# Two of five weight products of a transformer block taken from three fp32r passes to one fp32 pass

## The chip, the cores and the metric

The kernel runs on one core of a Trainium2 chip. Its engines work side by side, each through its own instructions in order: TensorE (PE in the profile, its weight loads PEld), VectorE (DVE), ScalarE (ACT), GpSimd (POOL), and SyncE (SP), which issues the DMAs. The metric is device microseconds (us) of one execution; less is better. Three runs of the kernel before took 1993.77, 1999.7 and 2000.05 us, so the median is 1999.7 us.

## The reference

The program is a block with modulated layer norms, 2048 tokens, width 512, all in fp32: attention with 32 heads of 16, then a mixer of two perceptrons with a token shift between its first two products. Cut to what matters:

```python
mod = (_silu(c) @ w_mod).reshape(c.shape[0], 6, 1, -1)
sa, ca, ga, sb, cb, gb = (mod[:, 0], mod[:, 1], mod[:, 2], mod[:, 3], mod[:, 4], mod[:, 5])
h = _layernorm(x) * (1 + ca) + sa
x = x + ga * attention(h, A_wqkv, A_wo)       # 32 heads of 16, softmax over 2048 keys
h = _layernorm(x) * (1 + cb) + sb
x = x + gb * mixer(h)

# mixer(x):
h = _gelu(_layernorm(x) @ w1)                 # 512 -> 512
g0, g1, g2, g3 = the four quarters of h's 512 columns, shifted by +1, -1, +2, -2 tokens
x1 = x + concatenate([g0, g1, g2, g3]) @ w2   # 512 -> 512
return x1 + _gelu(_layernorm(x1) @ w3) @ w4   # 512 -> 1792 -> 512
```

## The kernel before

**Attention.** The 2048 queries are taken in four chunks of 512. A chunk has 16 units (a unit is a pair of heads), and a unit has 16 steps, one for each 128 keys: 1024 steps in all. A step does two products for the scores (`sc`, line L1021), whose exponent ACT takes into the tile `pt` (L1017); two products for the row maxima of a unit that comes 24 steps later (`mb`, L1005), which DVE reduces (`mx`, L1001); a pass by POOL over `pt` that makes its low part (L1072, sometimes two halves on ACT instead); and the products with the values (`pv`, L1098 and L1095). Seven PSUM banks are shared by `sc`, `mb` and everything else but `pv`.

**The tail of a chunk** is all that follows attention: `tail(ci)`. It multiplies by `wo`, adds the residual, does two layer norms, then `mix1` (product with w1 and GELU into the tile `g1`), `mix2` (product with w2 over the token-shifted `g1`, the residual and a layer norm), and last the groups of `FG`: for each group of 128-column blocks of w3, the product with w3 and GELU into the tile `g2`, then for each 128-token tile one sum of products with w4 over the blocks of that group, which DVE adds to `x1` (L1535). A group's sum is one PSUM bank. Because of the shift by up to two tokens, the tail of chunk 0 finishes 3 token tiles, those of chunks 1 and 2 finish 4 each and that of chunk 3 finishes 5: 16 tiles. For each of these, w2 has 4 blocks and w4 has 14, so there are 16 x 18 = 288 products of 128x128 by 128x512 with w2 and w4.

**Three passes.** An fp32 product is made of three fp32r matmuls (`mm3`, L339, L341, L343) of operands that are split into a high and a low part: high by high, high by low, low by high. Activations are split behind the GELU: ACT rounds the GELU's result `xs` to the high part (L1427), POOL subtracts that for the low part (L1428). Weights are split once, while attention runs over the first chunk: `pieces_load` brings 40 tiles of 128x512 of wo, w1, w2, w3 and w4 from the inputs, `pieces_gen` scales them (w2 and w4 by 0.5, w4 also by a modulation row), splits them (ACT L900, POOL L902 or DVE L901), and stores both parts to `Ws`. A tail reads them back through `Ring`, three tiles `wr` of 1 MB ahead, 20 loads for each chunk.

**What sets the order.** `Sched` writes the instructions of all engines in one fixed order while the program is built, with its own clocks of the engines. Attention is written block by block of three pairs of row products. After every second block `fill` lets waiting generators (the tails, and during the first chunk the products for queries, keys and values) emit PE work, up to a budget of ns for each step: 900 and 700 in the first chunk, then the entries of `TAILB` for chunks 1, 2 and 3. So the tails of chunks 0, 1 and 2 are emitted between the blocks of attention of the following chunk, and the tail of chunk 3 comes after attention, alone. The list `chains` holds the elementwise work on ACT, DVE and POOL that belongs to a product; `misc` puts it between attention's own work on these engines. PE, DVE, ACT and POOL wait for each other by semaphores alone.

Of the kernel before, what the change touches and what calls it, by code (L numbers as in the profile page):

```python
# [15 lines left out]
OP = mybir.AluOpType  # L16
# [22 lines left out]
TAILB = (0.0, 500.0, 560.0, 590.0)  # L39
# [271 lines left out]
def kernel(ctx, tc, A_x, A_wqkv, A_wo, B_w1, B_w2, B_w3, B_w4, c, w_mod, out):  # L311
# [70 lines left out]
    FG = [(0, 4), (4, 4), (8, 4), (12, 2)]  # L382
# [93 lines left out]
    zero = con.tile([4, CH], F32, name="zero")  # L476
# [381 lines left out]
    def pieces_load():  # L858
        yield lambda: ("kq", 1) in done
        for i, (nm, src, nk, n) in enumerate(pieces):  # L860
# [12 lines left out]
    def pieces_gen():  # L873
        while True:
            yield lambda: loaded and wqs
# [4 lines left out]
            w = wqs.pop(0)  # L880
# [19 lines left out]
            sch.chain(*ops, ("A", cA(), lambda f=f, w=w: act.activation(w, f, AF.Copy)),  # L900
                      ("D", 2 * cD(), lambda f=f, t=t, w=w: dve.tensor_tensor(t, f, w, op=OP.subtract)) if nm in rows and c else  # L901
                      ("G", cG(), lambda f=f, t=t, w=w: pool.tensor_tensor(t, f, w, op=OP.subtract)),  # L902
                      (None, 0, store), ready=e)
# [58 lines left out]
    def load_unit(u):  # L962
# [4 lines left out]
        if u > 2:  # L967
            sch.dma(dma.dma_start, q[0::32].bitcast(F32), zero)
# [151 lines left out]
    def o_fin(u, ac, ready):  # L1120
# [9 lines left out]
        sm = at.tile([P, 8, DH + 1], F32, name="sm", tag="sm", bufs=1)  # L1130
        rc = at.tile([P, 8, 1], F32, name="rc", tag="rc", bufs=2)
# [22 lines left out]
    class Ring:  # L1154
# [9 lines left out]
        def add(self, n, pl=0):  # L1164

            for _ in range(n):
                if self.n < len(self.ids):
# [3 lines left out]
                    e = sch.dma(dma.dma_start, w.bitcast(F32), Ws[i])  # L1171
                    self.q.append((halves(w, pieces[i][2]), pl, e + WLAT))
# [50 lines left out]

    def cols_mm(b, w, i, A, n):
# [6 lines left out]
    def tail(ci):  # L1231
# [12 lines left out]
        if not rings:  # L1244
            ids = order["wo"] + order["w1"] + order["w2"]
            for f0, nf in FG:
                ids = ids + order["w3"][f0 // 2:(f0 + nf) // 2] + order["w4"][f0 // 2:(f0 + nf) // 2]
            rings.append(Ring(ids * NC))
# [18 lines left out]

        if ci:
# [139 lines left out]
        def gelu(b, n, hi, lo, key):  # L1408
            live.append(key)
            xs, sq = [tp[n > 2 * P].tile([P, 3 * P if n > 2 * P else 2 * P], F32, name=nm, tag=nm, bufs=XB) for nm in ("xs", "sq")]  # L1410
            xs, sq = xs[:, :n], sq[:, :n]
# [8 lines left out]
            def prod():  # L1420
                dve.scalar_tensor_tensor(xs, sq, 1.0, b, op0=OP.add, op1=OP.mult)  # L1421
# [4 lines left out]
                      ("D", cD(n), prod),  # L1426
                      ("A", cA(n), lambda: act.activation(hi, xs, AF.Copy)),  # L1427
                      ("G", cG(n), lambda: pool.tensor_tensor(lo, xs, hi, op=OP.subtract)), (None, 0, end), bank=b)  # L1428
# [274 lines left out]
```

## Time and profile before

| | |
|---|---|
| median of three runs | 1999.7 us (1993.77 to 2000.05) |
| profiled execution, span from first to last instruction | 2000.7 us, 1.0 us above the median |
| PE | 1920.9 us busy, 96% |
| POOL | 1676.1 us, 84% |
| DVE | 1652.2 us, 83% |
| ACT | 1473.6 us, 74% |
| DMA | 46.4% of 16 engines' time, 147 GB/s |
| granted TensorE clock, mean | 0.986 |

The profile gives no other time for the profiled execution than its span. PE's busy time is the time covered by at least one matmul from its start to its modelled end; matmuls overlap, so a stretch without a gap is not yet PE at its peak, and the distance from one start to the next tells more than the duration. L numbers are lines of the kernel; L339, L341 and L343 are the helper `mm3`, so there the tiles tell which product it is: `w<-wr,g` are w2 and w4, `w<-A,wr` are w1 and w3.

### The profile page before, as it was taken

The numbers are of one execution on the slowest core, as the hardware profiler recorded it, in microseconds if no ns is written. First come the engines' busy times: TensorE is split into PE (matmuls) and PEld (weight loads), VectorE is DVE, ScalarE is ACT, GpSimd is POOL, SyncE is SP. The second block draws the span as 40 slices with busy tenths as digits, with TensorE's granted clock in tenths as the row PEclk, the third lists the DMA queues.
The fourth block names the chain that finished last, engine by engine and source line by source line (L and its number), as shares of the span: only waits on it lengthen the run. The fifth ranks groups of instructions, "written<-read, shape, count | busy, mean of one in ns | idle before, by whom it ended". The sixth has DMA issues, their size and how long they took to land.

```text
span 2000.7 us, 42354 instructions
## 1 busy us (share of the span) xinstructions
PE 1920.9 (96%) x14480; PEld 1146.7 (57%) x14480; DVE 1652.2 (83%) x3010; ACT 1473.6 (74%) x3083; POOL 1676.1 (84%) x1609
## 2 busy tenths in 40 slices
PE   7999999999999999999999999999999999999899
PEld 4655555555455555555455555555555555555798
DVE  7887988888899888888989898898898889883643
ACT  5376888777878777777878787786787878777443
POOL 6287999889999998888999998898899989888532
PEclk8999999999999999999999999999999999999999
DMA  5767677766643334345433333334433343334432
GB/s 184 205 201 228 182 231 218 244 225 192 198 157 111 115 103 143 109 136 162 126 111 92 109 111 114 115 119 148 157 98 100 115 151 107 121 95 147 149 146 90
DMA packets 232352, 293.24 MB, mean 147 GB/s; under 512 B 125876, under 2 KB 177076, under 8 KB 215848
## 3 DMA queue, kind: packets, MB, share of 16 engines
q1 hardware_dynamic: 232136, 290.53, 46.4%
q8 instruction: 115, 1.88, 0.4%
q14 instruction: 101, 0.83, 0.1%
HBM read 225.81 MB, written 62.91 MB: 144 GB/s over the span
## 4 chain that ended last, share of the span: by engine, by line
PE 67%; DVE 16%; ACT 8%; issue 3%; POOL 2%; DMA 2%; SPq 1%; POOLq 0%; ACTq 0%; DVEq 0%
PE mb L1005 14%; PE sc L1021 10%; PE pv L1098 10%; DVE mx L1001 9%; PE w L339 7%; PE w L343 6%; PE w L341 6%; PE pv L1095 4%; ACT pt L1017 4%; POOL pt L1072 2%; DVE xs L1421 1%; DVE sq L1418 1%; DMA vst<-Vs 1%; PE mr L644 1%; PE ot L1127 1%
## 5 line engine op out<-in xcount | busy, mean ns | idle before, releaser
L1072 POOL TENSOR_SCALAR pt<-pt 128x1024 f16<-128x1024 uint16 x988 | 1312.5, 1365 | 132.6 <-ACT pt L1017 125.4
L1001 DVE TENSOR_REDUCE mx<-mb 128x1 f32<-128x512 f32 x2048 | 1281.0, 683 | 76.0 <-PE mb L1005 54.5
L1017 ACT ACTIVATE pt<-sc 128x512 int32<-128x512 f32 x2048 | 1090.8, 606 | 272.3 <-PE mb L1005 164.9
L1005 PE MATMUL mb<-kst,qtl 64*128 64x512 f32 x2048 | 752.1, 454 | 49.0 <-ACT pt L1017 16.1
L1021 PE MATMUL sc<-qtl,kst 64*128 64x512 f32 x2048 | 716.4, 444 | 2.6 <-DVE A L329 0.6
L1005 PEld LDWEIGHTS mb<-kst,qtl 64*128 64x128 f32 x2048 | 348.7, 193 | 254.5 <-DVE mx L1001 91.4
L1021 PEld LDWEIGHTS sc<-qtl,kst 64*128 64x128 f32 x2048 | 335.6, 186 | 153.5 <-DVE mx L1001 47.1
L1098 PE MATMUL pv<-pt,vst 128*32 128x512 f16 x4096 | 358.2, 397 | 0.1
L1095 PE MATMUL pv<-pt,vst 128*17 128x512 f16 (+1 forms) x2048 | 213.7, 394 | 2.2 <-POOL pt L1072 1.7
L1098 PEld LDWEIGHTS <-vst 128*32 128x32 bf16 x4096 | 90.9, 95 | 167.6 <-issue 108.8
L339 PE MATMUL w<-A,wr 128*128 128x256 f32 (+2 forms) x576 | 175.3, 304 | 0.3 <-ACT A L333 0.3
L1428 POOL TENSOR_TENSOR g<-xs,g 128x256 fp32r<-128x256 f32 (+2 forms) x144 | 103.2, 718 | 83.4 <-ACT g L1427 81.3
L341 PE MATMUL w<-A,wr 128*128 128x256 f32 (+2 forms) x576 | 169.8, 295 | 0.5 <-DVE A L329 0.3
L343 PE MATMUL w<-A,wr 128*128 128x256 f32 (+2 forms) x576 | 167.7, 291 | 0.0
L339 PEld LDWEIGHTS w<-A,wr 128*128 128x128 f32 x576 | 109.6, 190 | 35.4 <-DVE mx L1001 10.3
L339 PE MATMUL w<-wr,g 128*128 128x512 f32 x288 | 119.2, 414 | 0.6 <-ACT g L1427 0.6
L341 PEld LDWEIGHTS w<-A,wr 128*128 128x128 f32 x576 | 109.9, 191 | 12.4 <-issue 11.3
L343 PE MATMUL w<-wr,g 128*128 128x512 f32 x288 | 114.7, 398 | 0.2 <-POOL g L1428 0.2
L341 PE MATMUL w<-wr,g 128*128 128x512 f32 x288 | 113.6, 394 | 0.0
L343 PEld LDWEIGHTS w<-A,wr 128*128 128x128 f32 x576 | 109.8, 191 | 6.7 <-issue 6.7
L1535 DVE TENSOR_TENSOR x<-x,w 128x512 f32<-128x512 f32 x64 | 43.9, 687 | 82.0 <-PE w L343 82.0
L1424 ACT ACTIVATE sq<-w 128x256 f32<-128x256 f32 (+2 forms) x144 | 55.7, 387 | 68.8 <-PE w L343 66.0
(151 smaller groups left out, 2103.8 us busy)
## 6 DMA issues: line engine op xcount, KB each, us to landing
wr<-Ws SPq DMA_DIRECT2D x80, 1024.0 KB
kst<-Ks SPq DMA_DIRECT2D x189, 256.0 KB
vst<-Vs SPq DMA_DIRECT2D x252, 192.0 KB
qtl<-Qs SPq DMA_DIRECT2D x192, 64.0 KB
Vs<-vt SPq DMA_DIRECT2D x32, 384.0 KB
Ws<-wq SPq DMA_DIRECT2D x40, 256.0 KB
Ws<-wst SPq DMA_DIRECT2D x40, 256.0 KB
wst<-in_B_w_dram SPq DMA_DIRECT2D x36, 256.0 KB
```

Source lines behind the costliest of these rows:

```text
L339: te.matmul(o, lh, rh, start=first, stop=False)
L341: te.matmul(o, lh, rl, start=False, stop=False)
L343: te.matmul(o, ll, rh, start=False, stop=last)
L1001: end = sch.crit("D", 605, e + PX, lambda: dve.reduce_max(mxs[u][:, j, g, c:c + 1], b, axis=AX.X))
L1005: return ready, lambda: te.matmul(b, lhs, kst[u % 3][r, c * CH:(c + 1) * CH], start=True, stop=True), after
L1017: ea = sch.crit("A", 480, e + PX, lambda: act.activation(pt[s][:, j], b, AF.Exp))
L1021: return ready, lambda: te.matmul(b, kst[u % 3][r, kt * P:(kt + 1) * P], qst[u][r], start=True, stop=True), after
L1072: e_low[s] = XP["G"] + sch.crit("G", 1345, ready, lambda: pool.tensor_scalar(o, i, 0.5, 1.0, op0=OP.mult, op1=OP.mult))
L1095: te.matmul(acc[r:r + n, :], v[:, (kt + i) % 4, c - n:c].bitcast(F16), pt[s + i].bitcast(F16)[:, j, 0::2], start=False, stop=kt == NKT - 2 ...
L1098: te.matmul(acc[r:r + 32, :], v[:, kt % 4, r:r + 32], pt[s].bitcast(F16)[:, j, 1::2], start=kt == 0, stop=False, skip_group_check=True)
L1424: sch.chain(("A", cA(n), lambda: act.activation(sq, b, AF.Square)), ("D", cD(n), cube), ("A", cA(n), lambda: act.activation(sq, sq, AF.Tan ...
L1428: ("G", cG(n), lambda: pool.tensor_tensor(lo, xs, hi, op=OP.subtract)), (None, 0, end), bank=b)
```

## The change

The products with w2 and w4 become one fp32 matmul instruction in the program each (`plain_mm`, which advances the builder's clock by 3.75 times that of one 512-column fp32r matmul), over operands that are not split. GELU's last DVE operation writes straight into `g1` or `g2`; its copy on ACT and its subtraction on POOL are gone, and `g1` and `g2` hold one part where they held two. The weights of w2 and w4 are scaled, not split, and stored once; a ring load then holds four 128-row blocks where it held two, so a chunk takes 16 loads. The sums with w4 run over groups of 8 and 6 blocks, in the last chunk 4, 4 and 6, where they ran over 4, 4, 4 and 2. The entries of `TAILB` are 94 ns higher. Within a group, the w3 products of the token groups are taken in turn by pairs of blocks. Smaller edits: the tiles `sm` and `rc` behind attention have one buffer more, and the DMA that clears rows of a query tile reads a tile of 128 columns four times over. Products with wo, w1, w3, the queries, keys and values keep their three passes.

```diff
-TAILB = (0.0, 500.0, 560.0, 590.0)
+TAILB = (0.0, 594.0, 654.0, 684.0)
...
-    FG = [(0, 4), (4, 4), (8, 4), (12, 2)]
+    FG = [[(0, 8), (8, 6)]] * (NC - 1) + [[(0, 4), (4, 4), (8, 6)]]
+    PLAIN = ("w2", "w4")
...
-        for k0 in range(0, w.shape[0], 2 * P):
+        step = (4 if nm in PLAIN else 2) * P
+        for k0 in range(0, w.shape[0], step):
             order[nm].append(len(pieces))
-            pieces.append((nm, w[k0:k0 + 2 * P], 2, D))
+            x = w[k0:min(k0 + step, w.shape[0])]
+            pieces.append((nm, x, x.shape[0] // P, D))
...
-    zero = con.tile([4, CH], F32, name="zero")
+    zero = con.tile([4, P], F32, name="zero")
...
             def store(i=i, c=c, w=w, f=f, gone=gone, nm=nm):
-                for h, t in enumerate((w.bitcast(F32), f)):
-                    e = sch.dma(dma.dma_start, Ws[i][:, h, 512 * c:512 * c + 512], t)
+                if w is None:
+                    e = sch.dma(dma.dma_start, flat(Ws[i])[:, c], f)
+                else:
+                    for h, t in enumerate((w.bitcast(F32), f)):
+                        e = sch.dma(dma.dma_start, Ws[i][:, h, 512 * c:512 * c + 512], t)
...
-            if nm in ("w2", "w4"):
+            if plain:
                 ops.append(("A", cA(), lambda f=f: act.activation(f, f, AF.Copy, scale=0.5)))
-            sch.chain(*ops, ("A", cA(), lambda f=f, w=w: act.activation(w, f, AF.Copy)),
-                      ("D", 2 * cD(), lambda f=f, t=t, w=w: dve.tensor_tensor(t, f, w, op=OP.subtract)) if nm in rows and c else
-                      ("G", cG(), lambda f=f, t=t, w=w: pool.tensor_tensor(t, f, w, op=OP.subtract)),
-                      (None, 0, store), ready=e)
+            if not plain:
+                ops += [("A", cA(), lambda f=f, w=w: act.activation(w, f, AF.Copy)),
+                        ("D", 2 * cD(), lambda f=f, t=t, w=w: dve.tensor_tensor(t, f, w, op=OP.subtract)) if nm in rows and c else
+                        ("G", cG(), lambda f=f, t=t, w=w: pool.tensor_tensor(t, f, w, op=OP.subtract))]
+            sch.chain(*ops, (None, 0, store), ready=e)
...
-        sm = at.tile([P, 8, DH + 1], F32, name="sm", tag="sm", bufs=1)
-        rc = at.tile([P, 8, 1], F32, name="rc", tag="rc", bufs=2)
+        sm = at.tile([P, 8, DH + 1], F32, name="sm", tag="sm", bufs=2)
+        rc = at.tile([P, 8, 1], F32, name="rc", tag="rc", bufs=3)
...
+    def plain_mm(b, lhs, w, ks, nk):
+
+        for k in ks:
+            te.matmul(b, lhs(k), w[k // 4][:, k % 4], start=k == 0, stop=k == nk - 1)
+            yield 3.75 * nsq(CH)
...
-                pool.tensor_copy(g[:, k, :, 0:130], g[:, k, :, CH:CH + 130])
-            sch.chain(*[("G", 990, partial(copy, k)) for k in range(KT)], mark(("g", ci)))
+                pool.tensor_copy(g[:, k, 0:130], g[:, k, CH:CH + 130])
+            sch.chain(*[("G", 500, partial(copy, k)) for k in range(KT)], mark(("g", ci)))
...
-                dve.scalar_tensor_tensor(xs, sq, 1.0, b, op0=OP.add, op1=OP.mult)
+                dve.scalar_tensor_tensor(dst, sq, 1.0, b, op0=OP.add, op1=OP.mult)
                 sch.free(b)
...
-                      ("D", cD(n), prod),
-                      ("A", cA(n), lambda: act.activation(hi, xs, AF.Copy)),
-                      ("G", cG(n), lambda: pool.tensor_tensor(lo, xs, hi, op=OP.subtract)), (None, 0, end), bank=b)
+                      ("D", cD(n), prod), (None, 0, end), bank=b)
...
-                    yield from rows_mm(b, lambda k, p: g[:, k, p, 130 + (t - t0) * P - SH[k]:][:, :P], w, range(KT), KT)
+                    yield from plain_mm(b, lambda k: g[:, k, 130 + (t - t0) * P - SH[k]:][:, :P], w, range(KT), KT)
...
-                    yield from rows_mm(b, lambda k, p: g2[si][:, k, p, i * P:(i + 1) * P], w, range(nf), nf)
+                    yield from plain_mm(b, lambda k: g2[si][:, k, i * P:(i + 1) * P], w, range(nf), nf)
```

The builder's order moves with it. First, the tail of the third chunk (chunk 2), at a visit of PE to the sums with w4 between two blocks of attention, in the first group. `sc` and `mb` are attention's row products, `w` is the bank of the sum, `wr` the weights, `g` the tile g2. Before:

```order
L1005 MATMUL mb<-kst_153,qtl_151 128x512 x2
L1021 MATMUL sc<-qtl_605,kst_607 128x512 x2
L1005 MATMUL mb<-kst_153,qtl_151 128x512
L339 MATMUL w_24728<-wr,g_23769 128x512
L341 MATMUL w_24728<-wr,g_23769 128x512
L343 MATMUL w_24728<-wr,g_23769 128x512
```

The three last rows are one block of w4, and they come four times over in this visit, a whole sum of 4 blocks. Now, in the same tail and group:

```order
L1017 MATMUL mb<-kst_149,qtl_147 128x512
L1033 MATMUL sc<-qtl_770,kst_772 128x512 x2
L1017 MATMUL mb<-kst_603,qtl_601 128x512 x2
L1033 MATMUL sc<-qtl_770,kst_772 128x512
L1244 MATMUL w_24449<-wr,g_23008 128x512 x5
L1033 MATMUL sc<-qtl_770,kst_772 128x512
```

Five of the 8 blocks of one sum stand together, one instruction each, and the sum goes on in later visits.

Second, POOL in the same tail while `mix1` runs: its pass over `pt`, the subtraction for g1's low part (L1428), and small operations of attention (`nm`, `osb`). Before:

```order
L1428 TENSOR_TENSOR g_8517<-xs,g_8517 128x256
L1072 TENSOR_SCALAR pt_615<-pt_615 128x1024
L1072 TENSOR_SCALAR pt_616<-pt_616 128x1024
L1072 TENSOR_SCALAR pt_617<-pt_617 128x1024
L1428 TENSOR_TENSOR g_8517<-xs,g_8517 128x256
L1072 TENSOR_SCALAR pt_618<-pt_618 128x1024
```

Now, in the same stage of that tail:

```order
L1150 TENSOR_TENSOR osb<-sm,rc 128x4x32
L1084 TENSOR_SCALAR pt_613<-pt_613 128x1024
L1084 TENSOR_SCALAR pt_614<-pt_614 128x1024
L1084 TENSOR_SCALAR pt_615<-pt_615 128x1024
L1084 TENSOR_SCALAR pt_616<-pt_616 128x1024
L1084 TENSOR_SCALAR pt_609<-pt_609 128x1024
L1066 TENSOR_TENSOR nm<-mf,nm 128x8
```

The subtractions between the passes over `pt` are gone and nothing stands in their place.

Third, PE at the end of the program, where the last block of w3 (`A` by `wr`, 384 tokens) meets the last sums with w4. Before:

```order
L339 MATMUL w_29493<-A,wr 128x384
L341 MATMUL w_29493<-A,wr 128x384
L343 MATMUL w_29493<-A,wr 128x384
L339 MATMUL w_29513<-wr,g_29434 128x512
L341 MATMUL w_29513<-wr,g_29434 128x512
L343 MATMUL w_29513<-wr,g_29434 128x512
```

Behind these, the five tiles' sums take 2 blocks each, 30 matmuls. Now:

```order
L343 MATMUL w_28332<-A,wr 128x384
L1244 MATMUL w_28350<-wr,g_28133 128x512 x6
L1244 MATMUL w_28361<-wr,g_28133 128x512 x6
L1244 MATMUL w_28370<-wr,g_28134 128x512 x6
L1244 MATMUL w_28379<-wr,g_28134 128x512 x6
L1244 MATMUL w_28388<-wr,g_28134 128x512 x6
```

The five tiles' sums take 6 blocks each, 30 products; the two tiles whose GELUs come first (`g_28133`) stand ahead of the three that read the last GELU's tile (`g_28134`).

More of the change, by code (lines that the diff above doesn't have):

```diff
@@ L865, in pieces_load @@
             src3 = kpn(src)
-            for c in range(2):
+            for c in range(nk if nm in PLAIN else 2):
                 yield sch.wait(PLOAD)
                 yield lambda: len(wst) > WSR or len(ready) + ready["done"] > len(todo)
-                t, _, e = yield from staged([src3[:, c:c + 1] if nk == 2 else src3[:, 2 * c:2 * c + 2]])
+                t, _, e = yield from staged([src3[:, 2 * c:2 * c + 2] if n < D else src3[:, c:c + 1]])
                 loaded.append((i, nm, c, t, e))
@@ L874, in pieces_gen @@
         while True:
-            yield lambda: loaded and wqs
+            yield lambda: loaded and (loaded[0] is None or loaded[0][1] in PLAIN or wqs)
             x = loaded.pop(0)
@@ L879, in pieces_gen @@
             i, nm, c, t, e = x
-            w = wqs.pop(0)
+            plain = nm in PLAIN
+            w = None if plain else wqs.pop(0)
             f = t.bitcast(F32)
@@ L1244, in tail @@
         if not rings:
[L1245 to L1248, printed above, removed]
+            ids = []
+            for groups in FG:
+                ids += order["wo"] + order["w1"] + order["w2"]
+                for f0, nf in groups:
+                    ids += order["w3"][f0 // 2:(f0 + nf) // 2] + order["w4"][f0 // 4:(f0 + nf + 3) // 4]
+            rings.append(Ring(ids))
         ring = rings[0]
@@ L1493, in tail @@
             yield from mix1(0, grp[0])
-            w, more = yield from ring.get(2)
+            w, more = yield from ring.get(1)
             yield from mix2(0, sub[0])
@@ L1501, in tail @@
                 yield from mix1(gi, ts)
-            w, more = yield from ring.get(2)
+            w, more = yield from ring.get(1)
             for si, ts in enumerate(sub):
@@ L1505, in tail @@
         more()
-        for fi, (f0, nf) in enumerate(FG):
-            g2 = []
+        for fi, (f0, nf) in enumerate(FG[ci]):
+            g2 = [tG(nf, len(ts) * P) for ts in sub]
             w3 = []
-            for si, ts in enumerate(sub):
-                n = len(ts) * P
-                g2.append(tA("g2", n))
+            turns = [(fl, si) for fl in range(0, nf, 2) for si in range(len(sub))]
+            if end and not fi:
+                turns.sort(key=lambda x: x[1])
+            for fl, si in turns:
+                n = len(sub[si]) * P
                 yield lambda: ("T4", ci, si) in done
-                for fl in range(nf):
-                    if len(w3) <= fl // 2:
-                        w3.append((yield from ring.get(1)))
-                    (w,), more = w3[fl // 2]
+                if len(w3) <= fl // 2:
+                    w3.append((yield from ring.get(1)))
+                (w,), more = w3[fl // 2]
+                for i in range(2):
                     yield wait_bank
                     b = dbank("w3")
-                    yield from cols_mm(b[:, :n], w, fl % 2, An["xn4", si], n)
-                    gelu(b[:, :n], n, g2[si][:, fl, 0, :n], g2[si][:, fl, 1, :n], ("g2", ci, si, f0 + fl))
-                    if fl % 2 and si == len(sub) - 1:
-                        more()
-            w, more = yield from ring.get(nf // 2)
-            if fi == len(FG) - 1:
+                    yield from cols_mm(b[:, :n], w, i, An["xn4", si], n)
+                    gelu(b[:, :n], n, g2[si][:, fl + i, :n], ("g2", ci, si, f0 + fl + i))
+                if si == len(sub) - 1:
+                    more()
+            w, more = yield from ring.get((nf + 3) // 4)
+            if fi == len(FG[ci]) - 1:
                 done.add(("last", ci))
```

37 lines of the change are left out of this document (24 added, 13 removed).

## The prediction

> **What bounds the kernel now.** I read the page's head and its chain of waits first, to see which engine the end hangs on.
>
> ```profile
> span 2000.7 us, 42354 instructions
> PE 1920.9 (96%) x14480; PEld 1146.7 (57%) x14480; DVE 1652.2 (83%) x3010; ACT 1473.6 (74%) x3083; POOL 1676.1 (84%) x1609
> PE 67%; DVE 16%; ACT 8%; issue 3%; POOL 2%; DMA 2%; SPq 1%; POOLq 0%; ACTq 0%; DVEq 0%
> ```
>
> PE is covered for 96% of the span and holds two thirds of the chain. But 96% counts each matmul to its modelled end, so it hides short waits; and three other engines stand at 74 to 84%. So the second view is the table of windows, cut at the stages: attention over the four chunks, the latency stretch behind it, and the last tail.
>
> ```profile
> core 0: us, PE busy (x) PEld busy (x) DVE busy (x) ACT busy (x) POOL busy (x), PEclk, DMA share, GB/s
> 104.90:562.20 457.30, 436.90 (x3289) 242.54 (x3287) 384.04 (x653) 364.30 (x752) 408.09 (x347) 0.98 0.70 213
> 562.20:991.80 429.60, 415.86 (x3319) 234.73 (x3318) 377.47 (x699) 332.96 (x709) 383.14 (x371) 0.99 0.41 128
> 991.80:1422.00 430.20, 420.51 (x3353) 241.48 (x3356) 380.65 (x701) 336.53 (x705) 390.55 (x371) 1.00 0.37 115
> 1422.00:1845.80 423.80, 415.49 (x3313) 240.67 (x3312) 350.21 (x650) 332.38 (x697) 383.46 (x370) 1.00 0.38 119
> 1845.80:1892.00 46.20, 39.93 (x218) 32.47 (x215) 27.96 (x66) 19.27 (x41) 25.40 (x44) 0.93 0.43 162
> 1892.00:2000.70 108.70, 104.87 (x583) 94.01 (x581) 47.84 (x92) 40.32 (x91) 34.75 (x43) 1.00 0.33 120
> ```
>
> The last 109 us are PE alone: the others stand below half. In chunks 1 to 3 (562 to 1846), where the tails of chunks 0 to 2 run, POOL is at 0.89 to 0.91 and DVE at 0.83 to 0.88, so there the balance of four engines sets the pace. The third view, the waits, says what PE meets there.
>
> ```profile
> PEld mb L1005 <- DVE mx L1001: 91.4, 221, 3.8
> PEld mb L1005 <- ACT pt L1017: 82.0, 197, 1.4
> PE pv L1095 <- POOL pt L1072: 1.7, 3, 0.9
> ```
>
> Row products wait for banks that DVE's reductions and ACT's exponents give back; PE hardly ever waits for POOL directly.
>
> **The price of a product.** Three passes, from the timeline near the end, where PE is never held up:
>
> ```profile
> 1990.20 0.39 PE L339 MATMUL w<-wr,g 128*128 128x512 f32 x1
> 1990.43 0.39 PE L341 MATMUL w<-wr,g 128*128 128x512 f32 x1
> 1990.65 0.39 PE L343 MATMUL w<-wr,g 128*128 128x512 f32 x1
> 1990.88 0.39 PE L339 MATMUL w<-wr,g 128*128 128x512 f32 x1
> ```
>
> From start to start a pass takes 0.23 us, so a product 0.69. The kernel already has plain fp32 products, for other ends:
>
> ```profile
> 43.90 0.60 PE L795 MATMUL vb<-qk,gcol 128*128 128x256 f32 x2
> 44.33 0.60 PE L596 MATMUL tr<-ident,xt 128*128 128x128 f32 x4
> ...
> L795 PE MATMUL vb<-qk,gcol x16: 377/379/382, 41.1 to 188.1; 128*128 128x256 f32 x16
> ...
> L550 PE MATMUL mr<-wm,sil x16: 592/592/1057, 5.6 to 14.8; 128*1 128x512 f32 x16
> ...
> L339 PEld LDWEIGHTS w<-wr,g x288: 186/188/192, 676.2 to 1996.0; 128*128 128x128 f32 x144
> L339 PE MATMUL w<-wr,g x288: 387/393/507, 676.2 to 1996.2; 128*128 128x512 f32 x144
> ```
>
> The program calls L795 eight times (twice four blocks), and the profile has 16 records: one fp32 call is two matmuls on the engine. Two records of 256 columns take 44.33 - 43.90 = 0.43 us, so a call of 512 columns takes twice that, 0.86 us. L550 has the right width: its record lasts 592 ns against 387 for a pass of 512 columns, 205 more than 0.23, so 0.435, and a call 0.87. I take 0.864 us: **a product costs 0.174 us more than now**. A weight load takes 0.19 us and hides behind a record of 0.43.
>
> The Trainium skill, "Perfetto Trace Analysis", section Engine Utilization, gives TensorE half its output rate for FP32_LOW_HIGH, which read for a whole product would be 0.43 us; "FP8 and Floating Point Precision", section TensorE Precision Notes, gives a true fp32 product four passes. The trace agrees with four: two records, each at half rate. The first reading stays as a rival below.
>
> **The change part by part.** (1) *Products.* 288 x 0.174 = 50.1 us more on PE: 11 of the 16 token tiles lie between attention's blocks, 198 products or 34.5 us; 5 tiles lie in the last tail, 90 products or 15.7 us. What of the 34.5 us is paid? The table of windows again, for single units of attention, each 16 steps, of all engines and then of `w` alone (products with w1 to w4; none of wo fall into them), and of the transposes `xT`. Units alternate in length, since blocks of three row pairs do not divide a unit evenly, so like is compared with like: the four from 1215.8, 1318.0, 1368.0 and 1698.4 are even ones, those from 1561.9 and 1775.5 odd.
>
> ```profile
> 1318.00:1339.90 21.90, 21.82 (x200) 12.64 (x202) 20.47 (x39) 19.06 (x42) 21.34 (x21) 1.00 0.44 137
> 1368.00:1394.40 26.40, 26.34 (x206) 15.36 (x206) 20.73 (x36) 16.33 (x34) 19.13 (x16) 1.00 0.29 84
> 1561.90:1595.20 33.30, 31.22 (x248) 19.14 (x246) 28.00 (x53) 25.88 (x56) 32.83 (x32) 1.00 0.37 118
> 1775.50:1807.60 32.10, 31.91 (x232) 18.89 (x230) 25.22 (x45) 19.92 (x42) 24.67 (x22) 1.00 0.36 115
> ...
> 1215.80:1236.70 20.90, 3.39 (x24) 2.98 (x24) 0.83 (x2) 0.77 (x2) 1.00 0.53 174
> 1318.00:1339.90 21.90, 5.59 (x36) 4.59 (x36) 2.07 (x6) 1.16 (x3) 1.00 0.44 137
> 1368.00:1394.40 26.40, 11.00 (x48) 7.93 (x48) 2.06 (x3) 0.39 (x1) 1.00 0.29 84
> 1698.40:1726.00 27.60, 12.31 (x48) 8.62 (x48) 3.18 (x6) 0.00 (x0) 1.00 0.37 110
> 1561.90:1595.20 33.30, 12.06 (x72) 9.70 (x72) 4.33 (x10) 1.94 (x5) 1.00 0.37 118
> 1775.50:1807.60 32.10, 13.98 (x60) 10.23 (x60) 3.86 (x7) 0.39 (x1) 1.00 0.36 115
> ...
> 1561.90:1595.20 33.30, 1.09 (x8) 0.86 (x8) 1.97 (x3) 1.08 (x2) 1.00 0.37 118
> ```
>
> In the even units, from 3.39 to 5.59 us of `w` a unit grows by 1.0 us, 0.45 for each us: POOL at 0.97 and DVE at 0.93 pace it, and PE's extra work partly fills its waits. From 5.59 to 12.31 us it grows by 5.7, 0.85 for each us: with much `w` PE paces the unit, and DVE has fallen to 0.79. Sums with w4 make the full units, and the order shows them in longer visits (five blocks together, 4.3 us, where a visit held 2.8 us). So I take 0.85: **+29.3 us**; the bounds are 0.45 (15.5) and all of it (34.5).
>
> (2) *POOL and ACT.* The GELU loses its subtraction and its rounding.
>
> ```profile
> L1428 POOL TENSOR_TENSOR g<-xs,g 128x256 fp32r<-128x256 f32 (+2 forms) x144 | 103.2, 718 | 83.4 <-ACT g L1427 81.3
> L902 POOL TENSOR_TENSOR wst<-wst,wq 128x512 fp32r<-128x512 f32 x31 | 41.5, 1337 | 0.0
> L1535 DVE TENSOR_TENSOR x<-x,w 128x512 f32<-128x512 f32 x64 | 43.9, 687 | 82.0 <-PE w L343 82.0
> ```
>
> 108 of the 144 belong to tails under attention: 77 us of POOL, and as many roundings on ACT. The price comes from the two odd units above: 1561.9 has POOL at 0.99, 1775.5 at 0.77. The first is 1.2 us longer with 12.06 + 1.09 = 13.15 us of tail work on PE against 13.98; at 0.85 that makes 1.9 us for 8.2 us more of POOL (and the ACT and DVE work that comes with it), 0.23 for each us. 77 x 0.23: **-18 us**. Bounds: nothing, since PE waits 1.7 us for POOL by name; and half of the 77 paid in full, 38, since two of the four units shown with all engines have POOL at 0.97 or more.
>
> (3) *Weights in chunk 0.* By the order, POOL loses 11 subtractions of w2 and w4 tiles, 14.7 us, in a stage where it is at 0.89 (with 18 casts on ACT and 18 stores): at the same 0.23, **-3.4 us**; bounds 0 and 7.3, the same half.
>
> (4) *The last tail.* PE alone paces it, so 15.7 us are paid in full, both bounds alike. Two waits for split GELUs go:
>
> ```profile
> 1890.98 0.50 PE L339 MATMUL w<-wr,g 128*128 128x512 f32 x1 [0.61 <-ACT g L1427]
> 1993.77 0.50 PE L343 MATMUL w<-wr,g 128*128 128x512 f32 x1 [0.20 <-POOL g L1428]
> ```
>
> The first stands about 0.8 us later than the pace of 0.23 allows, the second 0.4, and two smaller ones beside them 0.2: -1.4. At the very end the order puts two tiles' sums of 6 blocks, 10 us, between the last w3 product and the first sum that needs the last GELU, so that wait stays hidden. **+14.3 us.**
>
> (5) *At nothing:* 27 sums fewer on DVE (0.69 us each), because they stand with w4, where DVE was at 0.79; without that cover 22 of them under attention would give 15 us at most, at (2)'s price 3.5. 16 ring loads and 18 stores fewer: DMA is at 0.37 to 0.41 in chunks 1 to 3, and no row of PE's waits names `wr`. Shorter copies of g1, the buffers of `sm` and `rc`, the clearing DMA in smaller pieces: below 1 us each. `TAILB` decides when tail work stands, not how much; earlier ends of a tail leave the last unit of a chunk without fill, which (1)'s upper bound covers.
>
> The sum: 29.3 - 18 - 3.4 + 14.3 = +22.2 on the profiled 2000.7, so 2022.9; that execution is 1.0 above the median, so **2022 us**.
>
> **The rivals.** *Full price.* Long fp32 visits starve DVE and ACT of banks to work on, nothing is absorbed, and POOL's relief is worth nothing as PE does not wait for it: 34.5 + 14.3 = +48.8, 2048 us. For it: the waits name DVE and ACT, whose work in attention stays. Against: 0.85 between even units, and the unit with POOL at 0.99.
>
> *The sides cancel.* Relief at 0.37 (28.5) and absorption midway at 0.65 (22.4), chunk 0 -5.4: +2.8, 2002 us.
>
> *Faster: POOL and DVE pace attention.* One mechanism: wherever POOL is at 0.97 or more, the next pass over `pt` is late and with it the blocks behind, though PE's wait is booked on ACT or DVE. Then 38 us come back, PE's addition is absorbed at 0.45 (15.5), chunk 0 gives 7.3: 15.5 - 38 - 7.3 + 14.3 = -15.5, 1984 us. It decides once units with w4 also stand below 6 us of `w`. For it: POOL's 0.89 to 0.91. Against: those are averages, and w4's units have POOL at 0.72 to 0.77.
>
> *Half the price.* A call is one half-rate pass, 0.43 us: 288 products save 0.26 each, 43 (at 0.85) + 23 us; with the other terms -90, 1910 us. Against it: two records for each call. That PE's order would not change is excluded by the order itself.
>
> **How the numbers follow.** Forecast 0.56 (its own range 2003 to 2041, from relief 28 with 0.65 to relief 8 with all paid), full price 0.13, cancel 0.14, faster 0.14, half price 0.03. The range 1998 to 2046 leaves out the two fast cases and the upper half of full price. A measurement here tells about 0.3%, 6 us, from no change: faster 0.14 + 0.03 = 0.17, same 0.14, slower 0.69.
>
> **What would show it.** Step price: L1244 with 576 records, 0.43 us from start to start; at 0.23 the half price holds. Stages: the last tail and the stretch before it, 154.9 us now, near 169; chunks 1 to 3 together 1283.6 now, near 1295 (1318 at full price, near 1261 if POOL paces); chunk 0 near 454. POOL in chunks 1 to 3 near 0.84. I am wrong if units with w4 grow by less than half of what w4 grows, or if the units around w3 and the layer norms shrink by more than 1 us each.

## The result: 3.4% slower

| kernel | median, us | lowest to highest | against before, 95% interval |
|---|---|---|---|
| before | 1999.9 | 1993.8 to 2001.2, 4 runs | |
| changed | 2067.1 | 2063.3 to 2069.2, 4 runs | 1.0339 [1.0323, 1.0356] |

The forecast was 2022 us, the range 1998 to 2046: the direction was right, the size was not. The move is 67 us where 22 were forecast.

**The profile after.** Its head, answering to the head of the page before:

```profile
span 2066.2 us, 41263 instructions
PE 1972.4 (95%) x14192; PEld 1094.4 (53%) x14192; DVE 1632.5 (79%) x2976; ACT 1420.4 (69%) x2919; POOL 1564.8 (76%) x1455
PE 69%; DVE 18%; ACT 7%; issue 2%; DMA 1%; POOL 1%; SPq 0%; ACTq 0%; POOLq 0%; DVEq 0%
```

PE gained 51.5 us of busy time, and the other three engines lost work. The span grew by 65.5, so more than PE's own work is in it: PE's share fell from 96 to 95%, though everything else has become lighter, and its idle time (span less busy) grew from 79.8 to 93.8 us.

The price of a product first: the group on the page, and the timeline near the end, where nothing holds PE up.

```profile
L1244 PE MATMUL w<-wr,g 128*128 128x512 f32 x576 | 271.5, 607 | 0.0
...
2053.80 8.75 PE L1244 MATMUL w<-wr,g 128*128 128x512 f32 x20
```

There are 576 records for 288 calls. Twenty of them take 8.75 us; without the modelled length of the last (0.59) that is 8.16 us for 19 distances, 0.43 us each, 0.86 for a call. That is the forecast's price. So what the title calls one pass is one instruction of the program, and two matmuls on the engine.

Then the windows by stage (columns as in the prediction), cut where attention's chunks and the last tail begin:

```profile
105.80:562.50 456.70, 436.18 (x3297) 243.37 (x3295) 378.47 (x647) 356.16 (x736) 394.17 (x337) 0.98 0.67 207
562.50:1007.10 444.60, 426.76 (x3257) 225.39 (x3256) 373.92 (x692) 321.99 (x669) 363.54 (x335) 0.99 0.35 110
1007.10:1458.00 450.90, 436.81 (x3297) 230.40 (x3296) 379.69 (x697) 326.83 (x670) 368.31 (x339) 1.00 0.34 105
1458.00:1897.20 439.20, 425.25 (x3216) 223.80 (x3219) 344.14 (x637) 322.06 (x661) 356.88 (x330) 1.00 0.32 100
1897.20:1958.00 60.80, 54.96 (x287) 40.22 (x280) 35.49 (x84) 22.03 (x45) 30.00 (x50) 0.94 0.37 137
1958.00:2066.20 108.20, 104.55 (x435) 70.50 (x433) 36.64 (x70) 23.60 (x54) 1.49 (x2) 1.00 0.16 58
```

Everything behind attention takes 60.8 + 108.2 = 169.0 us, as forecast. Chunk 0 is unchanged (456.7, was 457.3). Chunks 1 to 3 take 1334.7 us together where they took 1283.6: **+51.1, and 11 were forecast**. 40 of the 43 us by which the span misses its forecast are there. POOL stands at 0.82 in them, where 0.84 was forecast, so POOL was relieved as meant; what that is worth, experiment 3 shows. The waits, first of the kernel before, then of the changed one, say who waits:

```profile
ACT pt L1017 <- PE mb L1005: 164.9, 213, 2.5
POOL pt L1072 <- ACT pt L1017: 125.4, 134, 4.9
DVE mx L1001 <- PE mb L1005: 54.5, 105, 2.0
```

```profile
POOL pt L1084 <- ACT pt L1029: 262.2, 273, 6.4
ACT pt L1029 <- PE mb L1017: 260.6, 291, 3.8
DVE mx L1013 <- PE mb L1017: 143.3, 177, 3.5
```

ACT waits 96 us more for PE, DVE 89 more, and POOL 137 more for ACT: the rest stands behind PE. PE in turn waits a little more than before, by the 14 us of idle time above.

### The profile page after: what moved, and what is told of

It is laid out like the page before. It is cut to its first block, busy times and chain, and to the rows that moved or that the text cites. A ratio compares the mean times of both kernels' runs of the same rounds, so it can differ in the third digit from the quotient of the medians.

```text
span 2066.2 us, 41263 instructions
## 1 busy us (share of the span) xinstructions
PE 1972.4 (95%) x14192; PEld 1094.4 (53%) x14192; DVE 1632.5 (79%) x2976; ACT 1420.4 (69%) x2919; POOL 1564.8 (76%) x1455
## 4 chain that ended last, share of the span: by engine, by line
PE 69%; DVE 18%; ACT 7%; issue 2%; DMA 1%; POOL 1%; SPq 0%; ACTq 0%; POOLq 0%; DVEq 0%
PE mb L1017 14%; PE w L1244 12%; DVE mx L1013 11%; PE pv L1110 10%; PE sc L1033 9%; PE pv L1107 4%; ACT pt L1029 4%; PE w L339 3%; PE w L343 3%; PE w L341 3%; PE ot L1139 1%; DVE sq L1448 1%; DVE g L1451 1%; POOL pt L1084 1%; PE mr L650 1%
## 5 line engine op out<-in xcount | busy, mean ns | idle before, releaser
L1033 PEld LDWEIGHTS sc<-qtl,kst 64*128 64x128 f32 x2048 | 336.6, 186 | 181.5 <-ACT pt L1029 51.1
L1244 PE MATMUL w<-wr,g 128*128 128x512 f32 x576 | 271.5, 607 | 0.0
L1107 PE MATMUL pv<-pt,vst 128*25 128x512 f16 (+1 forms) x2048 | 212.9, 394 | 2.5 <-POOL pt L1084 2.3
L1244 PEld LDWEIGHTS w<-wr,g 128*128 128x128 f32 x576 | 101.7, 189 | 122.8 <-issue 113.4
L1448 DVE SCALAR_TENSOR_TENSOR sq<-sq,w 128x256 f32<-128x256 f32 (+2 forms) x144 | 60.0, 417 | 39.3 <-ACT sq L1454 38.1
L1455 ACT ACTIVATE sq<-sq 128x256 f32<-128x256 f32 (+2 forms) x144 | 60.0, 418 | 39.2 <-DVE sq L1448 39.2
L1451 DVE SCALAR_TENSOR_TENSOR g<-sq,w 128x256 f32<-128x256 f32 (+2 forms) x144 | 59.7, 416 | 34.4 <-ACT sq L1455 34.4
```

Of the source, the lines that this page charges most:

```text
L1033: return ready, lambda: te.matmul(b, kst[u % 3][r, kt * P:(kt + 1) * P], qst[u][r], start=True, stop=True), after
L1107: te.matmul(acc[r:r + n, :], v[:, (kt + i) % 4, c - n:c].bitcast(F16), pt[s + i].bitcast(F16)[:, j, 0::2], start=False, stop=kt == NKT - 2 ...
L1244: te.matmul(b, lhs(k), w[k // 4][:, k % 4], start=k == 0, stop=k == nk - 1)
L1448: dve.scalar_tensor_tensor(sq, sq, 1.0 / GELU_A, b, op0=OP.add, op1=OP.mult)
```

## The experiments

Two explanations stood against each other at the start, beside the recorded terms. In P, TensorE's price is paid in full, the relief is worth nothing, and the rest comes from the order of the work, above all from the higher budgets, which use up a tail early and leave the later units without tail work. In Q, the long fp32 visits themselves starve DVE and ACT, and the order is innocent. Later, G is the groups of 8 and 6 blocks, and Y the entries in the builder: that PE may turn to other work only behind a whole product, which counts for 3.75 passes.

| kernel | median, us | against before, 95% interval |
|---|---|---|
| 1. changed, products as three passes | 2024.3 | 1.0136 [1.0121, 1.0151] |
| 2. changed, old `TAILB` | 2059.0 | 1.0311 [1.0280, 1.0342] |
| 3. before, with the relief alone | 1993.4 | 0.9983 [0.9969, 0.9998] |
| 4. before, new `TAILB` | 2010.3 | 1.0069 [1.0049, 1.0089] |
| 5. as 1, old groups | 2009.5 | 1.0045 [1.0030, 1.0060] |
| 6. as 1, old groups, old `TAILB`, old entries | 1990.5 | 0.9945 [0.9927, 0.9963] |
| 7. as 1, old `TAILB`, old entries | 1994.0 | 0.9974 [0.9961, 0.9988] |
| 8. as 1, 3.75 entered in three parts | 2010.9 | 1.0049 [1.0033, 1.0065] |
| 9. changed, old groups, old `TAILB`, old count | 2032.4 | 1.0168 [1.0133, 1.0204] |
| 10. changed, old `TAILB`, old count | 2043.1 | 1.0230 [1.0196, 1.0263] |
| 11. before, `TAILB` 30 lower | 2008.4 | 1.0054 [1.0036, 1.0071] |
| 12. changed, 8 buffers for x | 2059.4 | 1.0300 [1.0263, 1.0337] |
| 13. before, 8 buffers for x | 1997.9 | 0.9996 [0.9981, 1.0010] |

Differences against the kernel before are taken from its runs beside the kernel in question: their medians are 1997.0 us for kernels 1 to 4, 1998.6 for 5 to 8, 1998.0 for 9 to 11 and 1999.7 for 12 and 13. Differences between two kernels of the table are of their medians; the ratios put some of them 2 to 4 us elsewhere. Kernel 3 leaves out the low part of the activations, kernels 1 and 5 to 8 that of w2 and w4 as well; these six have as many matmuls as the kernel before, and serve to time parts of the change.

**1. TensorE's price taken away, order kept.**

```diff
-            te.matmul(b, lhs(k), w[k // 4][:, k % 4], start=k == 0, stop=k == nk - 1)
+            for p in range(3):
+                te.matmul(b, lhs(k), w[k // 4][:, k % 4], start=k == 0 and p == 0, stop=k == nk - 1 and p == 2)
             yield 3.75 * nsq(CH)
```

(The tiles that these passes read are typed fp32r.)

> The changed kernel with its order of instructions kept, but each product with w2 and w4 made by three fp32r passes over the same unsplit operands (so the low parts are left out of the result and each product is counted three times). Only TensorE's price of a product moves, from 0.86 to 0.69 us, 288 times: 47 to 50 us. Theory P (TensorE's time is paid in full, the rest of the loss is the order with its higher budgets): 2067 - 48 = 2019 us, still 19 above the kernel before. Theory Q (long visits of TensorE to the fp32 sums starve VectorE and ScalarE; the order is innocent): the loss beyond the full price goes too, 2000 us or less. The prediction on record (0.85 of it paid under attention, all of it in the last tail): 2067 - 43 = 2024 us.

2024.3 us. TensorE's price is worth 42.8 in this order, of the 50.1 by which 288 calls are dearer, as the recorded prediction had it. By stage it is 28.9 us in chunks 1 to 3 (1334.7 against 437.0 + 439.9 + 428.9) and 13.8 behind attention (169.0 against 155.2). But 27 us above before remain with no price in it, where the relief should have put the kernel below it. So the order is not innocent.

**2 and 4. The budgets, both ways.**

```diff
-TAILB = (0.0, 594.0, 654.0, 684.0)
+TAILB = (0.0, 500.0, 560.0, 590.0)
```

> The changed kernel with the old budgets for work of the tails (500, 560, 590 ns a step in place of 594, 654, 684). Theory P: the tails spread again over the units that now stand empty at the end of each chunk, attention gets back most of the 19 us that it lost beyond TensorE's extra work: about 2050 us. Theory Q: budgets matter for nothing, 2067 us.

In the kernel before, the same edit the other way round:

> The kernel before with the new budgets alone (594, 654, 684). Theory P: tails are emitted earlier, the last units of each chunk stand without tail work, and attention gets longer by up to 19 us: 2010 to 2019 us. Theory Q: 2000 us.

2059.0: the changed kernel gains 8 us by the old budgets, about half of what P expected. 2010.3: the kernel before loses 13 by the new ones alone (10 against the runs of the result above), with the same matmuls and the same number of instructions on DVE; the builder only moved two passes over `pt` from POOL to four halves on ACT. What they do is seen in the last unit of chunk 2. In the kernel before, all engines and then the products with w1 to w4 alone:

```profile
1394.40:1422.00 27.60, 27.39 (x224) 15.58 (x226) 25.80 (x49) 22.64 (x50) 25.87 (x24) 1.00 0.53 174
...
1394.40:1422.00 27.60, 9.19 (x48) 6.56 (x48) 4.64 (x10) 1.17 (x3) 1.00 0.53 174
```

and the same unit with the new budgets:

```profile
1403.90:1427.20 23.30, 21.80 (x172) 10.31 (x170) 22.27 (x40) 19.75 (x42) 21.45 (x21) 1.00 0.57 180
...
1403.90:1427.20 23.30, 0.00 (x0) 0.00 (x0) 0.00 (x0) 0.00 (x0) 1.00 0.57 180
```

The tail was used up before. The unit lost 9.19 us of products and became only 4.3 us shorter: without tail work DVE is busy for 22.27 of its 23.30 us. The 9.19 us stand in earlier units now. If they are paid in full there, which these rows do not show, an empty last unit costs 9.19 - 4.3 = 4.9 us. By stage, chunk 1 takes 424.9 us with the new budgets (429.6 before), chunk 2 438.6 (430.2), and all behind it 586.0 (578.7): the loss begins in chunk 2. In chunk 1 the last unit stood empty before, too (see 12 and 13).

**3. The relief alone.** GELU's last DVE operation writes the high part directly, and all three passes read it.

```diff
-                dve.scalar_tensor_tensor(xs, sq, 1.0, b, op0=OP.add, op1=OP.mult)
+                dve.scalar_tensor_tensor(hi, sq, 1.0, b, op0=OP.add, op1=OP.mult)
...
-                      ("A", cA(n), lambda: act.activation(hi, xs, AF.Copy)),
-                      ("G", cG(n), lambda: pool.tensor_tensor(lo, xs, hi, op=OP.subtract)), (None, 0, end), bank=b)
+                      ("D", cD(n), prod), (None, 0, end), bank=b)
```

> The kernel before with three passes, old budgets and old groups, but without the GELU's rounding on ScalarE and subtraction on GpSimd: the product's three passes read the unsplit result in place of high and low part (so the low part of the activations is left out, and high by weights is counted again). TensorE's work is unchanged. Theory P (relief is worth nothing while TensorE's own matmuls and VectorE's reductions pace the blocks): 1997 to 2001 us. The prediction on record priced the relief at 18 us under attention and 1 us at the end: 1981 us.

1993.4, 0.0 to 0.3% below before: 3.6 us, where the forecast had 18 under attention and P nothing. Its page and waits:

```profile
PE 1910.8 (96%) x14480; PEld 1142.9 (57%) x14480; DVE 1648.6 (83%) x3010; ACT 1424.5 (71%) x2927; POOL 1590.6 (80%) x1471
...
POOL pt L1072 <- ACT pt L1017: 193.1, 247, 4.6
ACT pt L1017 <- PE mb L1005: 190.1, 248, 2.6
```

POOL has 85.5 us less to do and waits 67.7 us more for ACT, which waits 25 us more for PE. The engines behind PE became idler; the whole hardly became shorter.

**5 to 8. Groups and entries, without TensorE's price.** The four kernels are that of experiment 1 with these edits:

Kernels 5 and 6 have the old groups:

```diff
-    FG = [[(0, 8), (8, 6)]] * (NC - 1) + [[(0, 4), (4, 4), (8, 6)]]
+    FG = [[(0, 4), (4, 4), (8, 4), (12, 2)]] * NC
```

Kernels 6 and 7 have the old `TAILB`, and an entry of one pass behind each pass:

```diff
-TAILB = (0.0, 594.0, 654.0, 684.0)
+TAILB = (0.0, 500.0, 560.0, 590.0)
...
             for p in range(3):
                 te.matmul(b, lhs(k), w[k // 4][:, k % 4], start=k == 0 and p == 0, stop=k == nk - 1 and p == 2)
-            yield 3.75 * nsq(CH)
+                yield nsq(CH)
```

Kernel 8 has the groups and `TAILB` of the changed kernel, and enters the 3.75 in three parts:

```diff
-            yield 3.75 * nsq(CH)
+                yield 1.25 * nsq(CH)
```

> The three-pass kernel of the first experiment (each product with w2 and w4 as three single passes over the unsplit operands, so that PE pays no more than before; the output is not the reference's), with the groups of w3 and w4 blocks put back to 4, 4, 4 and 2; the higher TAILB and the entry of 3.75 passes after each whole product stay. That kernel stands 27 us above the kernel before with no price of a product in it; the budgets explain 8 to 13 of it, the relief takes 3.5 off, so 17 to 22 are open. Theory G (the groups of 8 and 6 blocks: GELUs in longer runs, sums in longer visits): 2024 - 18 = 2006, between 2002 and 2010. Theory Y (the coarse entries: the other work on PE gets its turn after a whole product, and a product uses up more of the budget): 2022, between 2018 and 2026.

> The same with everything of the order put back: old groups, old TAILB, and one entry after each pass as before, so that what is left of the change is the relief (no rounding, no subtraction, fewer weight tiles split, larger ring pieces). Both theories: 1993, between 1988 and 1998, as the run with the relief alone; above 2003, something that neither names (the larger ring pieces, chunk 0's loads) costs the difference.

> The three-pass kernel with old TAILB and one entry after each pass, so that of the order only the groups of 8 and 6 (with w3's products taken in turns) are new. G: 1993 + 18 = 2011, between 2006 and 2016. Y: 1994, between 1990 and 2000.

> The three-pass kernel with the changed kernel's groups and TAILB, but the 3.75 passes that a product counts entered in three parts, one after each pass, so that only the places where PE may turn to other work are finer. G: 2023, between 2019 and 2027. Y, if the length of the visits is what costs: 2008, between 2003 and 2013; if it is the count of 3.75 itself, as G.

Kernel 6 comes out at 1990.5, in the range of both: all the relief of the change, chunk 0's included, is worth 8 us (0.4 to 0.7%) as long as the order stays. From there the groups alone cost 3.5 (kernel 7), so G as a cause of its own falls in that order. The new budgets with the count of 3.75 cost 16.9 on top (7 to 8). Whole-product entries cost 13.4 on top of that (8 to 1), but the old groups take off as much (1 to 5: 14.7; 2009.5, where G said 2006 and Y 2022). So taking back either of the two undoes this last step. A good part of the step is one stall. PE's longest wait for a load of V in kernel 1, and the unit around it (the last of chunk 1, without tail work) in kernels 1 and 8:

```profile
977.01 0.79 PE L1017 MATMUL mb<-kst,qtl 64*128 64x512 f32 x2 [3.55 <-DMA vst<-Vs]
...
970.20:997.90 27.70, 23.09 (x168) 10.41 (x166) 21.77 (x39) 19.39 (x41) 21.34 (x19) 0.88 0.41 123
```

```profile
967.80:989.80 22.00, 20.69 (x168) 9.67 (x167) 21.69 (x39) 18.16 (x39) 21.00 (x19) 1.00 0.33 94
```

Kernels 5 and 8 have no such wait, and the unit takes 22.1 and 22.0 us there: 5.7 of the 13.4 us stand in this one unit (more under 12 and 13). Whether long groups and coarse entries cost anything else only together is not shown: old groups with an entry after each pass were not run with the new budgets.

**9 and 10. The fp32 products in the old order.**

```diff
-TAILB = (0.0, 594.0, 654.0, 684.0)
+TAILB = (0.0, 500.0, 560.0, 590.0)
...
-            yield 3.75 * nsq(CH)
+            yield 3 * nsq(CH)
```

and in kernel 9 also

```diff
-    FG = [[(0, 8), (8, 6)]] * (NC - 1) + [[(0, 4), (4, 4), (8, 6)]]
+    FG = [[(0, 4), (4, 4), (8, 4), (12, 2)]] * NC
```

> The changed kernel (fp32 products) with old groups, old TAILB, and a product entered as 3 passes as before: the change's arithmetic in nearly the old order. If the parts add up (three-pass kernel in the old order 1990.5, TensorE's price 42.8 as between the three-pass kernel of the first experiment and the changed kernel): 2033, between 2029 and 2038. If turning to other work only after a whole product, which a single fp32 call forces, costs its 13 here too (the first against the fine-entry kernel): 2046, between 2041 and 2051. If the price was only so high in the changed order, and the 0.85 of the recorded prediction is generous: under 2027.

> The changed kernel with its groups of 8 and 6, but old TAILB and a product entered as 3 passes: the ratio of budget to entry is as in the kernel before (and higher TAILB with 3.75 is nearly the same ratio, 594/3.75 against 500/3; all other tail work gets less a step). If the groups cost 3.5 as with fine entries: the run with old groups plus 3.5. If groups and whole-product visits together cost 14.7, as between the two three-pass kernels: plus 15.

2032.4 us, where the parts add up to 2033: the change's arithmetic costs 34 us in the old order, and turning to other work only behind a whole product costs nothing there, if TensorE's price is the same in both orders. The stages agree with that. Set against kernel 6, the same order without TensorE's price, chunks 1 to 3 and what lies behind them; kernel 6 first:

```profile
558.80:986.40 427.60, 412.93 (x3311) 232.50 (x3310) 377.02 (x698) 323.62 (x668) 364.10 (x335) 1.00 0.37 114
986.40:1415.70 429.30, 421.79 (x3361) 242.87 (x3360) 380.94 (x703) 325.77 (x667) 369.42 (x336) 1.00 0.35 105
1415.70:1833.50 417.80, 411.15 (x3296) 238.05 (x3298) 348.58 (x648) 320.47 (x657) 360.67 (x335) 1.00 0.35 107
1833.50:1988.00 154.50, 144.08 (x806) 127.62 (x798) 75.49 (x158) 45.32 (x96) 31.95 (x52) 0.98 0.28 103
```

```profile
556.50:990.50 434.00, 420.13 (x3257) 222.24 (x3256) 377.50 (x698) 323.00 (x668) 363.57 (x335) 0.99 0.37 113
990.50:1431.20 440.70, 431.40 (x3291) 228.86 (x3290) 383.05 (x704) 328.09 (x671) 367.83 (x335) 1.00 0.34 102
1431.20:1859.90 428.70, 421.72 (x3218) 224.36 (x3220) 348.33 (x645) 318.30 (x655) 361.98 (x336) 1.00 0.34 105
1859.90:2028.90 169.00, 159.69 (x720) 110.56 (x712) 76.06 (x159) 44.96 (x96) 30.60 (x51) 0.99 0.26 95
```

Under attention the products cost 1303.4 - 1274.7 = 28.7 us of the 34.5 by which they are dearer, 0.83 for each us; behind it 14.5 of 15.7. In the changed order it was 28.9 and 13.8.

Kernel 10 stands 10.7 above kernel 9, between the two expectations for the groups (3.5 and 15), and 24 below the changed kernel, from which it differs only in `TAILB` and the count. With the new `TAILB` and count, products with w2 and w4 get 5 to 7% less of a step (594 over 3.75 against 500 over 3 in chunk 1); all the other tail work gets 16 to 19% more, and the tail is used up sooner. The last two units of chunk 2 in the changed kernel, and in kernel 10 (all engines, then the last of them with w1 to w4 alone):

```profile
1409.90:1433.40 23.50, 22.79 (x172) 10.10 (x170) 19.63 (x35) 16.21 (x34) 18.66 (x17) 1.00 0.27 77
1433.40:1458.00 24.60, 22.25 (x180) 10.93 (x178) 22.97 (x41) 19.63 (x42) 23.51 (x24) 1.00 0.66 224
...
1433.40:1458.00 24.60, 0.00 (x0) 0.00 (x0) 0.00 (x0) 0.00 (x0) 1.00 0.66 224
```

```profile
1384.80:1409.30 24.50, 24.22 (x186) 11.86 (x184) 20.54 (x38) 17.36 (x37) 19.83 (x17) 1.00 0.39 116
1409.30:1446.10 36.80, 36.01 (x206) 15.23 (x204) 23.16 (x41) 18.64 (x38) 24.07 (x20) 1.00 0.26 82
...
1409.30:1446.10 36.80, 17.06 (x36) 6.35 (x36) 1.35 (x2) 0.00 (x0) 1.00 0.26 82
```

The last unit takes 24.6 us without any product, and 36.8 with 17.06 us of them: 12.2 us for 17.06, and again 4.9 us of products cost nothing in this unit. In the changed kernel the last unit of chunk 1 is empty too (below).

**11. Later still?**

```diff
-TAILB = (0.0, 500.0, 560.0, 590.0)
+TAILB = (0.0, 470.0, 530.0, 560.0)
```

> The kernel before with TAILB lowered by 30 (470, 530, 560). If earlier tail work costs because the last units of a chunk are left without it, a later tail fills them: faster, 1990 to 1997. If 500 already reaches to the chunk's end, the tail runs into the next drain in one block: 2005 or more.

2008.4: slower as well, in the range of the second expectation. Of the three settings tried, that of the kernel before is the best: 30 ns a step less cost 10 us, 94 more cost 13. The trace does not settle why the later tail loses: chunk 1 takes 429.1 us (429.6 before), chunk 2 434.0 (430.2), and chunk 0, which the edit does not touch, 460.1 (457.3). No version tried is faster than the kernel before with the reference's arithmetic.

**12 and 13. A stall behind SP.** Part of what the changed order costs has another face. In the changed kernel, the longest wait of PE for a load of V, SP's waits for stores of the result, and the windows of the last unit of chunk 1 and of stretches in it:

```profile
985.99 0.80 PE L1017 MATMUL mb<-kst,qtl 64*128 64x512 f32 x2 [3.05 <-DMA vst<-Vs]
...
SPq L106 <- DMA out_dram<-x: 12.3, 2, 6.7
...
979.70:1007.10 27.40, 23.30 (x168) 10.65 (x166) 21.80 (x39) 19.42 (x40) 21.31 (x19) 0.88 0.41 123
...
984.00:990.00 6.00, 4.01 (x27) 1.65 (x29) 1.54 (x4) 0.60 (x1) 2.94 (x3) 0.62 0.46 150
990.00:996.00 6.00, 5.73 (x40) 2.88 (x36) 5.59 (x10) 5.22 (x12) 3.46 (x4) 0.81 0.06 3
996.00:1002.00 6.00, 5.71 (x55) 2.56 (x53) 5.27 (x9) 5.34 (x11) 5.51 (x5) 1.00 0.26 68
```

The same unit of the kernel before, empty too:

```profile
968.60:991.80 23.20, 21.66 (x172) 10.27 (x170) 22.21 (x40) 19.68 (x42) 21.38 (x21) 1.00 0.58 183
```

It takes 27.4 us against 23.2. The loads of the next x stand on SP until the store of the last result has landed, and loads of V stand behind them. PE waits 3 us, and its granted clock is 0.62 over the 6 us around the wait's end and 0.81 over the next 6. Cut into single us, it is 0.50 from 986 to 992 and 1.00 from 993 on. So more buffers for x, with every engine's order unchanged:

```diff
-                d = x1t[t] = tp[0].tile([P, D], F32, name="x1", tag="x1", bufs=5)
+                d = x1t[t] = tp[0].tile([P, D], F32, name="x1", tag="x1", bufs=8)
```

> The changed kernel, instruction for instruction in the same order on every engine, with 8 buffers for the rows x where it has 5, so that a chunk's x loads no longer wait on SP for the store of the chunk before. In the changed kernel SP waits 12.3 us in two places for such a store, and behind the first stand the loads of V for the last unit of chunk 1: that unit takes 27.4 us without any tail work, 22.0 in the three-pass kernel with fine entries, which has no such wait. If that wait is what the late V costs: 2067.1 - 5.4 = 2062, between 2059 and 2064. If V would have been late anyway (the queue itself is slow there): 2067, within 2.

> The kernel before with the same 8 buffers. Its SP waits 6.3 us in two places for a store, but PE nowhere waits for a load of V or K behind it. If only a wait that reaches PE costs: 1998, within 3. If the stalled queue costs in other ways (kst, qtl, weights later): 1993.

2059.4 (2053.6 to 2065.7) is in the range of the first expectation, but the interval of its ratio overlaps that of the changed kernel. The trace says more than the time. PE's wait for V, SP's wait for weights between 955 and 995 us, and windows:

```profile
979.30 0.50 PE L1017 MATMUL mb<-kst,qtl 64*128 64x512 f32 x2 [2.29 <-DMA vst<-Vs]
...
SPq L106 <- DMA wr<-Ws: 3.7, 2, 2.4
...
962.00:968.00 6.00, 5.72 (x56) 2.86 (x48) 6.00 (x12) 4.72 (x10) 5.84 (x7) 1.00 0.85 288
968.00:974.00 6.00, 5.49 (x52) 2.86 (x55) 5.74 (x11) 5.43 (x12) 6.00 (x8) 1.00 0.89 342
...
980.00:986.00 6.00, 5.80 (x49) 2.43 (x48) 4.01 (x8) 3.37 (x9) 2.17 (x3) 0.74 0.16 41
```

SP's wait for the store is gone (0.2 us are left) and V is still late: the unit went from 27.4 to 26.1 us, the last unit of chunk 2 lost 1.6, and 5.5 of the 9 us between the two spans lie in a unit of chunk 0 (33.1 and 27.6 us), before any store of a result. So little of the 8 us between the medians can be put down to the buffers. But SP's wait has in the main moved: it now waits 3.7 us for weight tiles to land where it waited 5.6 for the store, and from the issue of the two weight tiles to that of V's next load it takes 13.5 us (962.24 to 975.69), where it took 14.1 (968.17 to 982.30). So the edit did not bring V's load forward, and what an earlier load would be worth stays open. In view besides is the burst just before: the tail's early end calls for two weight tiles of 1 MB and 1 MB of x at once with the K and V of the next unit, 288 to 342 GB/s at a DMA share of 0.85 to 0.89. Whether that burst alone makes V late was not tried. In the kernel before, the buffers change nothing, as the first expectation had it, where no wait for V reaches PE.

## Why the prediction was wrong, point by point

Along the kernels, from the order of before to the changed one: relief -8, groups +3.5, budgets with the count of 3.75 +16.9, entries behind whole products +13.4 (with the long groups; 5.7 of it in the unit with the late V), TensorE's price +42.8. Each step starts where the one before ends, so that they add up to about the measured 67 is no check of them.

- **The price of a product was right**: 0.864 us forecast, 0.86 in the changed kernel. The prediction weighed two rules of the Trainium skill; the trace agrees with "FP8 and Floating Point Precision", section TensorE Precision Notes (four passes for a true fp32 product), in that a call is two records of 0.43 us where one fp32r pass takes 0.23, so 3.7 passes' time.
- **(1), 0.85 for each us under attention, was right**: 0.83 between kernels 6 and 9, 28.7 us against 29.3, and 28.9 in the changed order.
- **(4), the last tail, was right in its sum**: 169.0 us as forecast. Its two parts were each off by about 1 us, and it is luck that they cancel: the products cost 14.5 between kernels 6 and 9 where 15.7 were forecast, and the waits that go brought 0.4 (154.9 to 154.5 in kernel 6) where 1.4 was forecast.
- **(2), POOL's relief at 0.23 for each us, 18 us, failed**: 3.6 by kernel 3, and in kernel 6 chunks 1 to 3 are 8.9 shorter (1283.6 to 1274.7). The price came from two units that differed in more than POOL's load, and the difference that carried it was 1.9 us. POOL at 0.99 in one of them was read as a pace; kernel 3 shows POOL waiting for ACT in place of the work taken off. The lower bound that the prediction gave, nothing, with its reason (PE waits 1.7 us for POOL by name), was the better reading.
- **(3), chunk 0**: with 3.4 forecast, it takes 451.0 us in kernel 9, 454.2 in kernel 6, 456.7 in the changed kernel and 457.3 before. It scatters by as much as the term.
- **(5), the order at nothing, failed, and it is the larger failure.** "`TAILB` decides when tail work stands, not how much" is true, but when it stands decides how much of it is covered: the last unit of chunk 2 became only 4.3 us shorter by 9.19 us of products. The prediction named the empty last unit and covered it with (1)'s upper bound, 5 us above the value taken; the budgets cost 13 us in the kernel before and 24 in the changed one with their count. Of the 24, the empty unit of chunk 2 gives 4.9 us if its products are paid in full elsewhere, and the unit with the late V in chunk 1 4.2 (27.4 - 23.2); the remaining 15 us were not put down to single units. Chunks 1 to 3 at 1334.7 us lie above the full price's 1318, so no rival had this term either.
- **The rival of the full price** (2048) had the relief right (nothing), the absorption wrong (0.83, not 1), and put the blame on long fp32 visits starving DVE and ACT. Kernel 9 has the same fp32 calls, and stands where the parts add up. So the long visits as a cause fall in the old order, and kernel 1 shows that the new order costs without fp32 calls too.

With the terms as measured, 8 for all of the relief and nothing for the order, the forecast's own sum gives 28.7 + 14.5 - 8 = +35, 2035 us. That is near the 2032 of kernel 9 because the terms were read from kernels 6 and 9. The rest up to 2067, 32 to 35 us, is the order.

## What to carry to other kernels

Where two engines pace a loop in turns, a stretch of it can have room for other work (here 4.9 us of PE time beside DVE's reductions in the last unit of chunk 2, in two pairs of kernels): an edit that moves that work can cost by the places it leaves empty, though no matmul is added. So budgets and costs in a builder's order are terms of the sum, to be priced by a stretch with and one without the work, and an arithmetic change is best timed in the old order first. An engine at 0.99 in one stretch is not yet the pace: look at what waits for it by name.

## What was not expected of the hardware

A call in fp32 over 512 columns costs two matmul records at 0.43 us from start to start, so it is 0.17 us dearer than the three fp32r passes it replaces. Around the end of a wait of PE of 3.05 us the granted clock went to 0.50 for some 6 us, and of one of 2.29 us in kernel 12 for some 3 us. In kernel 1 the unit around such a wait, of 3.55 us, took 5.7 us more than in kernel 8, more than the wait itself. That the wait is what halves the clock is not shown: from 1057.0 to 1060.4 us the changed kernel has 0.51 too, and from 1050 on PE waited no longer than 0.45 us there.
